# Attention scores and values on packed 32-wide TensorE tiles, in one burst per head, in place of whole-array matmuls spread among the projections

## The chip, the cores and the metric

The kernel runs on one core of one Trainium2 chip. The metric is device time in microseconds (us); lower is better. Executions of one kernel agree within about 0.2%. A profile is one execution taken by the hardware profiler. Its engines are PE (TensorE matmuls), PEld (TensorE weight loads, which overlap PE), DVE (VectorE), ACT (ScalarE), POOL (GpSimd) and SP (SyncE). `L630` is line 630 of that kernel's source, so the same statement has different line numbers in the two kernels. All runs told here were in the fast state, with the mean granted TensorE clock at 0.99 to 1.00. The 0.99 belongs to one experiment, in whose attention stage the clock halved for short stretches; this is told there.

## The reference, cut to what matters

```python
# S = 2048 tokens, 1024 wide; attention A: 32 heads of 128, segments of 32 tokens, 8 memory tokens; gated unit B: F = 3584
xn = layernorm(x)
s = A(xn, mem0, ...)     # per segment of 32: h = [mem (8), xs (32)]; q, k, v = h Wq, h Wk, h Wv
                         # p = softmax(mask(q k^T * scale)); o = p v; o Wo; its first 8 rows are the next memory
g = silu(B(xn, ...))     # (sigmoid(x w_gate) * (x w_up)) w_down
return x + s * g
```

The kernel does not run the 64 segments one after the other. It estimates the memories first, handles all segments at once, and checks at the end whether its estimate was good enough (a flag; if not, a sequential version follows). So a segment's attention is a causal 32x32 score block for its own keys, plus a memory term that is added to the values (`vm`) and to the denominator (a constant 8). The first segment keeps its own small 40x40 attention.

## The kernel before

For each head, TensorE computes q and k of all tokens: 2 x 5 blocks of about 411 columns, each with 8 matmuls, 80 in all ("projections", tile `pr`). The attention of the head before is spread among them. Four segments of 32 tokens share a 128x128 score matmul. Three quarters of its output lie outside the segments and are masked to zero.

```python
psb = es_p.enter_context(tc.tile_pool(name="psb", bufs=4, space=PSUM))     # shared matmul buffers, one bank each
...
        def s_steps(h, i):                                                  # scores: 16 matmuls a head, in batches of 4
            ...
            for j in range(n):
                o = M + (j0 + j) * P
                nc.tensor.matmul(s_ps[:, j * P:(j + 1) * P], lhsT=kt[:, o:o + P], rhs=qt[:, o:o + P], start=True, stop=True)
                if j < n - 1:
                    yield
            pv = pT[:, j0 * P:(j0 + n) * P]
            nc.scalar.activation(pv, s_ps[:, 0:n * P], ACTF.Exp, scale=scale)
            pv = pv.rearrange("p (a b) -> p a b", b=P)
            nc.vector.tensor_tensor(pv, pv, mask[:].unsqueeze(1).to_broadcast([P, n, P]), op=ALU.mult)
            yield

        def pv_steps(h, i):                                                 # values: 16 matmuls a head, 3 to a PSUM bank
            ...
            for j in range(n):
                o = (j0 + j) * P
                nc.tensor.matmul(o_ps[:, j, :], lhsT=pT[:, o:o + P], rhs=va[:, j0 + j, v0:v0 + OW],
                                 start=True, stop=True)                     # OW = 130: 128 values and ones for the denominator
            last = j0 + n == NT
            if last:                                                        # the first segment's own attention
                nc.tensor.matmul(o_ps[:, n, :], lhsT=pT[:, S:S + P], rhs=va[:, NT, v0:v0 + OW], start=True, stop=True)
            ...                                                             # VectorE: + vm, reciprocal, product, into osb

        for h in range(H + 1):                                              # cut
            for i in range(NSL):                                            # NSL = 80 projection matmuls
                ...
                if pj is not None:
                    next(pj, None)                                          # one projection matmul of head h
                if at is not None:
                    next(at, None)                                          # a step of the attention of head h - 1
```

After the last output tile, this kernel also runs 114 small matmuls on 32- and 64-wide tiles whose results nobody reads. They are a test of packed tiles that was left in:

```python
        X, Y, Z = wo_sb[:, 0, :], wo_sb[:, 1, :], wo_sb[:, 2, :]
        for _ in range(2):
            ...                                # 16 matmuls on 128x32 tiles (32 columns), 8 on 128x64 tiles (64 columns)
        ...
        for t in range(3):
            for c in range(4):
                for r in range(4):             # 48 matmuls on 32x32 tiles, 130 columns
                    q = slice(r * SEG, (r + 1) * SEG)
                    nc.tensor.matmul(pbs[r][c * SEG:(c + 1) * SEG, t * OW:(t + 1) * OW], lhsT=X[q, t * P + c * SEG:t * P + (c + 1) * SEG],
                                     rhs=Y[q, c * P:c * P + OW], start=True, stop=True)
```

## Time and profile before

| | before |
|---|---|
| median, us | 1582.82 (1582.62 to 1583.65, 4 runs) |
| span of the profile, us | 1581.1 |
| PE busy | 99% |
| distance of two heads in the attention stage, us | 15.79 |
| of this, 80 projections at 173.7 ns | 13.90 |
| attention matmuls of one head, us | 1.89 |
| last output matmul's start to the end, us | 8.40 |

The profile's page starts with the busy time and share of each engine.

```profile
PE 1567.0 (99%) x9353; PEld 808.9 (51%) x9456; DVE 708.5 (45%) x1252; ACT 539.7 (34%) x1087; POOL 162.4 (10%) x302
```

Its part on the chain that ended last gives shares of the span by engine, then by engine and line:

```profile
PE 99%; issue 0%; POOL 0%; ACT 0%; DVE 0%; POOLq 0%
PE pr L630 28%; PE a_ps L899 14%; PE v_ps L368 14%; PE y_ps L889 12%; PE u_ps L173 12%; PE g_ps L169 12%; PE o_ps L671 2%; PE s_ps L651 2%; PE acc L424 1%; PE vm_ps L533 1%; PE vm_ps L562 0%; PE pt L342 0%; PE o_ps L675 0%; POOL mx L434 0%; POOL mx L433 0%
```

The table by stretches of time shows that this holds inside the attention stage too: in 495 us PE is busy for all but 0.05 us, while VectorE and ScalarE have a quarter of their time or more to spare.

```profile
core 0: us, PE busy (x) PEld busy (x) DVE busy (x) ACT busy (x) POOL busy (x), PEclk, DMA share, GB/s
325.00:820.00 495.00, 494.95 (x3567) 302.95 (x3566) 361.39 (x688) 282.56 (x593) 57.22 (x107) 1.00 0.54 136
```

The timeline of PE in that stage (start in us, us, then the merged instructions) shows how attention is spread among projections. From one start to the next, two projections and one score take 0.40 us: 2 x 174 ns and 56 ns. Matmuls overlap, so durations (0.22 us for one score) must not be added. Starts are what counts.

```profile
612.82 0.22 PE L651 MATMUL s_ps<-qt,kt 128*128 128x128 bf16 x1
612.88 0.51 PE L630 MATMUL pr<-xnT,wqk 128*128 128x412 bf16 x2
613.23 0.22 PE L651 MATMUL s_ps<-qt,kt 128*128 128x128 bf16 x1
613.29 0.33 PE L671 MATMUL o_ps<-va,pT 128*128 128x130 bf16 x3
613.46 0.51 PE L630 MATMUL pr<-xnT,wqk 128*128 128x410 bf16 x2
```

At the end stands the left-over test. The timeline again; `128*32` and `32*32` are the tile shapes:

```profile
1572.84 0.28 PE L945 MATMUL pa<-wo_sb 128*32 128x32 bf16 x16
...
1573.05 0.32 PE L950 MATMUL pa<-wo_sb 128*64 128x64 bf16 x8
...
1574.69 0.60 PE L967 MATMUL pb<-wo_sb 32*32 32x130 bf16 x48
```

The starts of its single matmuls, read from the trace's records, price the packing:

```
128x32 tiles, 32 columns, ns from the first:  0 3 7 10 | 38 42 45 49 | 63 67 70 74 | 88 92 95 100
32x32 tiles, 130 columns, ns from the first:  0 3 6 10 ... 50 | 67 70 ... 117 | 252 261 269 277 ... 377
```

### The profile page before, as it was taken

Reading aid. Unit: us, or ns where it says so; the run is one execution under the profiler, and the core shown is the slowest. Engines: PE = TensorE matmul, PEld = TensorE weight load, DVE = VectorE, ACT = ScalarE, POOL = GpSimd, SP = SyncE. Lnnn points to the kernel's source line nnn. Section 1 sums busy time; section 2 is a strip of 40 time slices with the busy share of each in tenths; the row PEclk is TensorE's granted clock in tenths of the full one; section 3 lists DMA queues with packets and bytes.
Section 4 is the critical chain, followed back from the end, with each engine's and each line's share of the span. In section 5 each row is a group of like instructions: output and inputs, shape, how many; then the busy total and the mean of one; then the engine's idle time right before and its main releaser. Section 6 shows DMA issues by size and latency. Waiting matters only on the chain.

```text
span 1581.1 us, 22861 instructions
## 1 busy us (share of the span) xinstructions
PE 1567.0 (99%) x9353; PEld 808.9 (51%) x9456; DVE 708.5 (45%) x1252; ACT 539.7 (34%) x1087; POOL 162.4 (10%) x302
## 2 busy tenths in 40 slices
PE   9999999999999999999999999999999999999998
PEld 4444445566666666666654444444444444444444
DVE  6555534357777777777773112121223333311211
ACT  4555552155555555555541111111111122100000
POOL 2111110101101110111011101111100000000000
PEclk9999999999999999999999999999999999999999
DMA  7744654856564655455524353523253334343430
GB/s 228 206 140 140 207 187 141 247 129 156 157 166 124 157 158 139 108 142 148 112 61 147 129 184 127 201 79 98 62 136 104 93 117 107 103 122 88 109 102 29
DMA packets 257790, 212.99 MB, mean 135 GB/s; under 512 B 83528, under 2 KB 219848, under 8 KB 257680
## 3 DMA queue, kind: packets, MB, share of 16 engines
q1 hardware_dynamic: 229904, 140.40, 34.0%
q0 software_dynamic: 17200, 56.37, 10.0%
q10 hardware_dynamic: 10576, 14.70, 3.0%
q8 instruction: 76, 1.25, 0.3%
q14 instruction: 34, 0.28, 0.1%
HBM read 129.06 MB, written 63.50 MB: 122 GB/s over the span
## 4 chain that ended last, share of the span: by engine, by line
PE 99%; issue 0%; POOL 0%; ACT 0%; DVE 0%; POOLq 0%
PE pr L630 28%; PE a_ps L899 14%; PE v_ps L368 14%; PE y_ps L889 12%; PE u_ps L173 12%; PE g_ps L169 12%; PE o_ps L671 2%; PE s_ps L651 2%; PE acc L424 1%; PE vm_ps L533 1%; PE vm_ps L562 0%; PE pt L342 0%; PE o_ps L675 0%; POOL mx L434 0%; POOL mx L433 0%
## 5 line engine op out<-in xcount | busy, mean ns | idle before, releaser
L630 PE MATMUL pr<-xnT,wqk 128*128 128x412 bf16 (+1 forms) x2560 | 500.6, 337 | 0.0
L630 PEld LDWEIGHTS <-wqk 128*128 128x128 bf16 x2560 | 222.4, 97 | 134.3 <-issue 0.4
L899 PE MATMUL a_ps<-wo_sb,ot 128*128 128x512 bf16 (+2 forms) x1037 | 225.0, 372 | 1.0
L368 PE MATMUL v_ps<-wv_sb,xnT 128*128 128x512 bf16 x1002 | 222.2, 379 | 1.8 <-ACT xnT L344 0.7
L173 PE MATMUL u_ps<-xnT,wu 128*128 128x512 bf16 x879 | 210.3, 379 | 1.0
L169 PE MATMUL g_ps<-xnT,wg 128*128 128x512 bf16 x870 | 209.3, 379 | 1.3
L177 DVE SCALAR_TENSOR_TENSOR hst<-th,u_ps 128x512 bf16<-128x512 f32 x112 | 77.0, 687 | 286.5 <-PE u_ps L173 273.5
L889 PE MATMUL y_ps<-wd,ht 128*128 128x512 bf16 x877 | 197.2, 379 | 1.0
L176 ACT ACTIVATE th<-g_ps 128x512 f32<-128x512 f32 x112 | 67.0, 598 | 300.5 <-PE g_ps L169 287.0
L899 PEld LDWEIGHTS <-ot 128*128 128x128 bf16 x1056 | 102.1, 98 | 119.3
L368 PEld LDWEIGHTS <-xnT 128*128 128x128 bf16 x1024 | 99.4, 98 | 118.4 <-ACT xnT L344 1.2
L173 PEld LDWEIGHTS <-wu 128*128 128x128 bf16 x896 | 87.7, 98 | 105.7
L889 PEld LDWEIGHTS <-ht 128*128 128x128 bf16 x896 | 87.1, 98 | 105.3 <-issue 1.2
L169 PEld LDWEIGHTS <-wg 128*128 128x128 bf16 x896 | 86.7, 98 | 101.5
L680 DVE TENSOR_TENSOR of<-o_ps,vm 128x387 f32<-128x387 f32 x192 | 98.8, 515 | 42.5 <-PE o_ps L671 29.4
L633 ACT CAST kt<-pr 128x412 bf16<-128x412 f32 (+1 forms) x160 | 80.0, 500 | 92.9 <-PE pr L630 92.6
L655 ACT ACTIVATE pT<-s_ps 128x512 bf16<-128x512 f32 x128 | 76.4, 597 | 102.0 <-PE s_ps L651 101.1
L371 ACT CAST v_sb<-v_ps 128x512 bf16<-128x512 f32 x128 | 74.9, 585 | 104.9 <-PE v_ps L368 101.4
L651 PE MATMUL s_ps<-qt,kt 128*128 128x128 bf16 x512 | 110.4, 219 | 0.0
L892 ACT ACTIVATE th<-y_ps 128x512 f32<-128x512 f32 x32 | 19.1, 597 | 234.7 <-PE y_ps L889 234.7
L905 DVE SCALAR_TENSOR_TENSOR tmp<-a_ps,gq 128x512 f32<-128x512 f32 (+2 forms) x33 | 22.3, 675 | 166.7 <-PE a_ps L899 166.5
L633 ACT CAST qt<-pr 128x412 bf16<-128x412 f32 (+1 forms) x160 | 79.5, 497 | 27.5 <-PE pr L630 27.5
(165 smaller groups left out, 1155.6 us busy)
## 6 DMA issues: line engine op xcount, KB each, us to landing
vp_dram<-v_sb POOLq DMA_DIRECT2D x64, 256.0 KB, 3.3
va<-vp_dram SPq DMA_DIRECT2D x16, 1024.0 KB
o_dram<-osb POOLq DMA_DIRECT2D x16, 960.0 KB, 11.6
hT_dram<-hst POOLq DMA_DIRECT2D x56, 256.0 KB, 3.9
ht<-hT_dram SPq DMA_DIRECT2D x16, 896.0 KB, 5.1
vm<-vm_dram SPq DMA_DIRECT2D x48, 256.0 KB, 11.7
xt<-in_A_x_dram SPq DMA_DIRECT2D x32, 256.0 KB, 4.3
wo_t<-in_A_Wo_dram ACTq DMA_DIRECT2D x8, 1024.0 KB, 5.7
```

The costliest lines, as they stand in the source:

```text
L169: nc.tensor.matmul(g_ps[:], lhsT=wg[:, c, fc * P:(fc + 1) * P], rhs=xnT[:, c, tb * TB:(tb + 1) * TB], start=(c == 0), stop=(c == KC - 1))
L173: nc.tensor.matmul(u_ps[:], lhsT=wu[:, c, fc * P:(fc + 1) * P], rhs=xnT[:, c, tb * TB:(tb + 1) * TB], start=(c == 0), stop=(c == KC - 1))
L177: nc.vector.scalar_tensor_tensor(hst[:, :, fc, :], th[:].rearrange("p (a b) -> p a b", b=P), 1.0, u_ps[:].rearrange("p (a b) -> p a b", b= ...
L368: nc.tensor.matmul(v_ps[:], lhsT=xnT[:, c, t * P:(t + 1) * P], rhs=wv_sb[:, c, cg * 512:(cg + 1) * 512], start=(c == 0), stop=(c == KC - 1))
L371: nc.scalar.copy(v_sb[:, j * 512:(j + 1) * 512], v_ps[:])
L630: nc.tensor.matmul(pr[:, 0:b - a], lhsT=w_[:, c, hc], rhs=xmT[:, c, a:b], start=(c == 0), stop=(c == KC - 1))
L633: nc.scalar.copy(dst[:, a:b], pr[:, 0:b - a])
L651: nc.tensor.matmul(s_ps[:, j * P:(j + 1) * P], lhsT=kt[:, o:o + P], rhs=qt[:, o:o + P], start=True, stop=True)
L655: nc.scalar.activation(pv, s_ps[:, 0:n * P], ACTF.Exp, scale=scale)
L680: nc.vector.tensor_tensor(of[:, o:o + n, :], o_ps[:, 0:n, f:f + DH + 1], vm[:, j0:j0 + n, v0 + f:v0 + f + DH + 1], op=ALU.add)
L889: nc.tensor.matmul(y_ps[:], lhsT=hts[t][:, c, :], rhs=wd[:, c, hf * 512:(hf + 1) * 512], start=(c == 0), stop=(c == FC - 1))
L899: nc.tensor.matmul(a_ps[:], lhsT=ox[t][0][:, h, :], rhs=wo_sb[:, h, a:b], start=(h == 0), stop=(h == H - 1))
```

## The change

Its intent is to stop paying for the three quarters of each score matmul that are masked away. Segments are regrouped so that four of them (one from each quarter of the tokens) stand in the four 32-row groups of one 128x512 tile. Scores run on 128x32 column tiles, four at a time. Values run on 32x32 tiles, sixteen at a time. Exponentials and masks then touch 512 columns a head in place of 2048. All attention matmuls of a moment stand together in one burst: the scores of head h-1 and the values of head h-2, after the eighth projection of head h. Denominators get matmuls of their own (four of 4 columns). The value output takes four PSUM banks, so the shared buffers fall from four to three. The left-over test goes. Some loads move, and the memory term is loaded from a rearranged copy in larger packets.

```diff
-    psb = es_p.enter_context(tc.tile_pool(name="psb", bufs=4, space=PSUM))
+    psb = es_p.enter_context(tc.tile_pool(name="psb", bufs=3, space=PSUM))
...
+        def scores(h):
+            ...
+            xs = xss["s"] = psb.tile([P, 512], F32, name="xs", tag="big")
+            nc.tensor.matmul(xs[:, 0:L], lhsT=kt[:, 0:P], rhs=qt[:, 0:L], start=True, stop=True)
+            s_ps = ps.tile([P, PW], F32, name="s_ps", tag="s")
+            for t in range(NT):
+                for a in range(4):
+                    o = M + a * 4 * P + t * SEG
+                    nc.tensor.matmul(s_ps[a * SEG:(a + 1) * SEG, t * SEG:(t + 1) * SEG], lhsT=kt[:, o:o + SEG],
+                                     rhs=qt[:, o:o + SEG], start=True, stop=True)
...
+        def values(h):
+            ...
+            o_ps = ps.tile([P, 4, 4, DH], F32, name="o_ps", tag="o")
+            for q in range(4):
+                for c in range(4):
+                    t = 4 * q + c
+                    for a in range(4):
+                        r = slice(a * SEG, (a + 1) * SEG)
+                        nc.tensor.matmul(o_ps[c * SEG:(c + 1) * SEG, a, q, :], lhsT=pT[r, t * SEG:(t + 1) * SEG],
+                                         rhs=va[r, t, hc], start=True, stop=True)
+            xs = xss["v"] = psb.tile([P, 512], F32, name="xs", tag="big")
+            den = xs[:, 0:NT].rearrange("p (a q) -> p a q", q=4)
+            for q in range(4):
+                nc.tensor.matmul(den[:, :, q], lhsT=pT[:, q * P:(q + 1) * P], rhs=bones[:], start=True, stop=True)
+            nc.tensor.matmul(xs[:, P:P + OW], lhsT=pT[:, PW:PW + P], rhs=vx[:, v0:v0 + OW], start=True, stop=True)
...
-        for h in range(H + 1):
+        for h in range(H + 2):
...
+                if i == KC:
+                    if 0 < h <= H:
+                        scores(h - 1)
+                    if h > 1:
+                        values(h - 2)
+                    if 0 < h <= H:
+                        weights(h - 1)
+                    if h > 1:
+                        outputs(h - 2)
+                    if 0 < h <= H:
+                        causal(h - 1)
...
-            y_ps = psb.tile([P, 512], F32, name="y_ps", tag="big")
+            y_ps = ps.tile([P, 512], F32, name="y_ps", tag="y", bufs=2)
...
-        X, Y, Z = wo_sb[:, 0, :], wo_sb[:, 1, :], wo_sb[:, 2, :]
-        ...                                     (the whole left-over test)
```

## The prediction

> **What bounds the kernel.** TensorE. The page gives PE 99% of the 1581.1 us span, and the chain of waits is 99% PE. In the attention stage (table by stretches, 325 to 820 us) PE is busy 494.95 of 495.00 us at clock 1.00; DVE 361 and ACT 283 are not limits. So only PE time counts. Cheaper DVE masking, fewer exponentials and larger vm packets are off the critical path.
>
> **What attention costs PE now.** In the timeline one head takes 15.79 us start to start. Its 80 projection matmuls are 173.7 ns apart: 13.90 us. The other 1.89 us is attention: 16 score matmuls (56 ns apart), 17 value matmuls (57 ns), one 128x40 (26 ns).
>
> **What the change does.** Per head, one burst replaces these: a 128x40 matmul; 64 score matmuls on 128x32 column tiles, 32 columns each; 64 value matmuls on 32x32 tiles, 128 columns each; four 4-column denominator matmuls; one 130-column matmul. The kernel before ends with a probe of just such tiles, and its timeline prices them:
> - 128x32 tiles, 32 columns: four start within 10 ns, the next four 25 ns later. 64 cost about 0.41 us.
> - 32x32 tiles, 130 columns: 32 start within 117 ns, then 135 ns of nothing, then one each 8.3 ns. I read this as a full queue of 64 instructions that empties, then a dispatch limit near 4.15 ns per instruction.
> - Changing tile shape costs about 100 ns each time (106 to 149 ns between starts, against 25 to 55 within a shape). The Trainium skill ("TensorEngine Tiling (Array Packing)", Tiling Modes) says a change of mode drains the engine; this trace agrees. A burst has three changes.
>
> Estimate of a burst: 0.03 + 0.12 + scores 0.41 + 0.06 (queue empty) + 0.05 (dispatch) + 0.11 + values 0.43 + 0.14 + denominators 0.11 + 0.06 = 1.52 us. So 1.52 us replaces 1.89 us: 0.37 us a head, 12 us over 32 heads. The small pairs are bound by dispatch and three drains.
>
> **Tail.** The probe goes. Its PE work runs from 1572.84 to 1575.3 us. PE alone then reads the flag and branches (4.27 us), and the last barrier waits for that, so the probe is on the critical path: 2.3 us saved. The output DMA lands by 1574.7 us, early enough.
>
> **Other.** Three projection buffers instead of four: matmul groups take 1.4 to 1.7 us, copies 0.5 to 0.7 us, so no waits. Each head's chain now stretches over three heads, leaving slack. I allow 1 us for a stall at the stage's start, where the memory layout moves.
>
> **Prediction: 1569 us, 80% range 1561 to 1577.** Chances: faster by over 2% 0.03, within 2% 0.94, slower by over 2% 0.03.
>
> **What would show it.** Heads 15.4 us apart; PE still 99%; projections still 174 ns apart; bursts near 1.5 us with three gaps near 0.1 us; score tiles 6 to 8 ns apart on average, value tiles about 8 ns once the queue is empty; DVE and ACT busy less without effect; last PE matmul followed directly by the branch.
>
> **What would make it wrong.** Instruction fetch: a burst has about 270 instructions and the program is fetched in 16 KB pieces taking 1 to 2 us; starving would push bursts over 2 us and eat the gain. Faster dispatch than 8.3 ns a pair would bring bursts to 1.2 us (1559 us). Waits on the single score and output buffers, or a projection buffer held by VectorE, would appear as gaps after the burst.

## The result, and the profile after

| | before | after |
|---|---|---|
| median, us | 1582.82 (1582.49 to 1584.96, 12 runs) | 1569.42 (1568.86 to 1570.14, 8 runs) |
| span of the profile, us | 1581.1 | 1568.4 |
| distance of two heads, us | 15.79 | 15.45 |
| attention matmuls of one head, us | 1.89 | 1.54 |
| last output matmul's start to the end, us | 8.40 | 5.86 |

The ratio is 0.9914 (95% interval 0.9904 to 0.9924). Ratios here are the mean time of one kernel's fast runs over that of the other's of the same rounds, so they are not quite the ratio of the medians quoted. The change is 0.9% faster, which is clear of noise.

PE is still the only limit. The page's engine line, and the chain:

```profile
PE 1553.2 (99%) x12438; PEld 789.2 (50%) x12542; DVE 641.5 (41%) x964; ACT 492.4 (31%) x991; POOL 152.9 (10%) x299
```

```profile
PE 98%; DVE 1%; DMA 1%; issue 0%; ACT 0%; SPq 0%
```

The table by stretches: the same full PE, with nearly twice the matmuls, and 60 us less VectorE and 44 us less ScalarE.

```profile
325.00:820.00 495.00, 494.89 (x6772) 290.99 (x6773) 301.46 (x416) 239.06 (x504) 49.21 (x110) 1.00 0.57 138
```

The timeline of PE over one burst, with the projections left out, and the start of the next head's burst:

```profile
512.29 0.18 PE L652 MATMUL xs<-qt,kt 128*128 128x40 bf16 x1
512.40 0.66 PE L657 MATMUL s_ps<-qt,kt 128*32 128x32 bf16 x64
513.00 0.73 PE L685 MATMUL o_ps<-va,pT 32*32 32x128 bf16 x64
513.66 0.26 PE L690 MATMUL xs<-bones,pT 128*128 128x4 bf16 x4
513.78 0.22 PE L691 MATMUL xs<-vx,pT 128*128 128x130 bf16 x1
...
527.74 0.18 PE L652 MATMUL xs<-qt,kt 128*128 128x40 bf16 x1
```

The starts of the single matmuls of one such burst, from the trace's records:

```
ns from the burst's start
small whole-array matmul   0
scores, 64                 112 ... 590     first four within 10 ns, then four each 25 ns; from the 33rd on one each 8.4 ns
values, 64                 705 ... 1215    first 31 within 141 ns; the 33rd 251 ns after the first; then one each 8.3 ns
denominators, 4            1370 ... 1460
first segment              1485
next projection            1541
```

Where the 12.7 us of the two profiles went, by starts on PE:

| stretch | before, us | after, us | difference |
|---|---|---|---|
| start to last value projection | 238.28 | 238.53 | +0.25 |
| from there to the first q/k projection | 73.34 | 73.91 | +0.57 |
| first to last q/k projection | 503.34 | 491.76 | -11.58 |
| from there to the first output matmul (last heads, gated unit) | 340.49 | 341.06 | +0.57 |
| first to last output matmul | 417.24 | 417.24 | 0.00 |
| last output matmul to the end | 8.40 | 5.86 | -2.54 |

The fourth line belongs to attention as well: the values of the last head now follow the projections. So attention gave 11.0 us, which is 0.344 us a head. The tail gave 2.5 us, and 0.8 us came on before the stage. The first line varies from run to run: in the changed kernel run again it was 239.17 us, because that run's first loads came later (the view of waits has 1.8 us for a load of `wv_sb`, against 0.3 us).

The second line has a new wait. The view of waits (engine and line, what it waited for, us in total, times, longest) lists it for the kernel after. The kernel before has no such line.

```profile
PE g_ps L169 <- DVE hst L177: 0.4, 1, 0.4
```

### The profile page after: what moved, and what is told of

Read it like the earlier page. It is cut to its first block, busy times and chain, and to the rows that moved or that the text cites. A ratio compares the mean times of both kernels' runs of the same rounds, so it can differ in the third digit from the quotient of the medians.

```text
span 1568.4 us, 28695 instructions
## 1 busy us (share of the span) xinstructions
PE 1553.2 (99%) x12438; PEld 789.2 (50%) x12542; DVE 641.5 (41%) x964; ACT 492.4 (31%) x991; POOL 152.9 (10%) x299
## 4 chain that ended last, share of the span: by engine, by line
PE 98%; DVE 1%; DMA 1%; issue 0%; ACT 0%; SPq 0%
PE pr L641 28%; PE a_ps L916 14%; PE v_ps L372 14%; PE y_ps L906 12%; PE u_ps L173 12%; PE g_ps L169 12%; PE o_ps L685 1%; PE s_ps L657 1%; PE acc L433 1%; PE vm_ps L542 0%; DMA wv_sb<-in_A_Wv_dram 0%; PE vm_ps L571 0%; PE xs L690 0%; DVE svT L391 0%; DMA xt<-in_A_x_dram 0%
## 5 line engine op out<-in xcount | busy, mean ns | idle before, releaser
L641 PE MATMUL pr<-xnT,wqk 128*128 128x412 bf16 (+1 forms) x2560 | 450.2, 337 | 0.0
L641 PEld LDWEIGHTS <-wqk 128*128 128x128 bf16 x2560 | 248.2, 97 | 191.0 <-issue 0.4
L710 DVE TENSOR_TENSOR osb<-of,rden 128x1024 bf16<-128x1024 f32 x64 | 78.4, 1225 | 2.1
L624 DVE TENSOR_TENSOR mx<-mx,ab 128x2048 bf16<-128x2048 bf16 x64 | 78.2, 1222 | 1.2
L709 DVE TENSOR_TENSOR of<-o_ps,vm 128x1024 f32<-128x1024 f32 x64 | 77.5, 1211 | 0.0
```

The source lines that it names most:

```text
L624: nc.vector.tensor_tensor(mx[:, x, :], mx[:, x, :], abs_.pop((h, x))[:], op=ALU.max)
L641: nc.tensor.matmul(pr[:, 0:b - a], lhsT=w_[:, c, hc], rhs=xmT[:, c, a:b], start=(c == 0), stop=(c == KC - 1))
L709: nc.vector.tensor_tensor(of[:], o_ps[:, 2 * i:2 * i + 2].rearrange("p a q d -> p (a q) d"), vm[:, x, hc], op=ALU.add)
L710: nc.vector.tensor_tensor(osb[:, x, hc], of[:], rd[:, x].unsqueeze(2).to_broadcast([P, 8, DH]), op=ALU.mult)
```

## The experiments

All ten kernels gave results within tolerance, even the one ("only the scores packed") whose denominators belong to other segments on purpose. Three (the tail alone, the work given back, values ahead of scores) were timed together with the changed kernel run again, on the same chip, so it and the kernel before of that group (1582.94 us) are their yardsticks. The others ran in two more groups on two other chips, where the kernel before took 1583.18 and 1582.82 us; they are held against the changed kernel's 1569.42 us.

### The changed kernel again

> The changed kernel again, unedited, as the yardstick of this group of runs. Expected 1569.4 us within 1 us. It also tells whether the start of the program, where its profile was 0.25 us behind the kernel before by the end of the value projections, varies from run to run.

Measured: 1569.53 us (1568.78 to 1571.28, 5 runs), ratio to before 0.9917 (0.9904 to 0.9931). The last value projection started at 239.17 us, against 238.53 in the first profile. Over the twelve profiles told here it lies between 238.13 and 240.42 us, so the start alone can move one profile by up to 2 us. Heads were 15.45 us apart and bursts 1.540 us, as in the first profile.

### The tail alone

```diff
 # the kernel before
-        X, Y, Z = wo_sb[:, 0, :], wo_sb[:, 1, :], wo_sb[:, 2, :]
-        ...                                     (the whole left-over test)
```

> The kernel before, without the packed test matmuls at its end. Theory (TensorE alone reads the flag, branches and releases the last barrier, so the test is on the critical path): the time falls by 2.3 to 2.6 us, to about 1580.4 us. Rival (the last output transfer would end as late anyway): it falls by under 0.5 us. The two profiles put the step from the last output matmul to the end at 8.40 us before and 5.86 us after, 2.54 us less; if this kernel shows about 5.9 us, the tail is explained by the test alone.

Measured: 1580.03 us (1579.58 to 1580.48, 5 runs) against 1582.94 us, 2.9 us less; ratio 0.9982 (0.9968 to 0.9995). From the last output matmul to the end its profile has 5.42 us. The test was on the critical path, and the rival falls. The trace's records of the kernel before show why: TensorE reads the flag at 1575.05 us, when its last test matmul starts, and its branch then takes 4.27 us. SyncE has finished its waits for transfers by 1575.2 us and then stands in the last barrier (4.26 us in one wait) until TensorE arrives.

### VectorE and ScalarE given their work back

```diff
 # the changed kernel; scr and scd are scratch tiles of 128x512
+                if i in (26, 38, 48, 56, 68) and 0 < h < H:
+                    if i < 50:
+                        nc.scalar.activation(scr[:], scr[:], ACTF.Exp, scale=scale)
+                    nc.vector.tensor_tensor(scd[:], scd[:], scd[:], op=ALU.mult)
```

> The changed kernel with useless work given back to VectorE (five 128x512 multiplies a head, about 2 us) and ScalarE (three 128x512 exponentials a head, about 1.8 us), as much as the change took from them. Theory (they are off the critical path): the time stays at 1569.4 us within 1 us, heads stay 15.45 us apart, and the busy times of VectorE and ScalarE in the attention stage return to about 360 and 290 us. Rival (part of the gain came from relieving them): at least 3 us slower.

Measured: 1569.62 us (1568.84 to 1569.65, 5 runs), ratio to before 0.9915. Heads are 15.44 us apart. Its table by stretches shows the work back at 357 and 288 us, with PE unmoved:

```profile
325.00:820.00 495.00, 494.89 (x6771) 290.86 (x6772) 356.81 (x572) 288.26 (x597) 49.41 (x110) 1.00 0.57 138
```

So none of the gain came from the fewer exponentials and masks.

### Only the scores packed

```diff
 # the changed kernel
-                    o = M + a * 4 * P + t * SEG
+                    o = M + t * P + a * SEG
...
+            for a in range(4):                      # spread the masked weights block-diagonally (VectorE)
+                r = slice(a * SEG, (a + 1) * SEG)
+                nc.vector.tensor_copy(bds[h % 2][r, :, r], pv[r])
...
-            for q in range(4):                      # 64 value matmuls on 32x32 tiles
-                ...
+            for t in range(NT):                     # 16 value matmuls on the whole array
+                nc.tensor.matmul(o_ps[:, t // 4, t % 4, :], lhsT=bds[h % 2][:, t, :], rhs=va[:, t, hc], start=True, stop=True)
```

(The values are also loaded in natural order, in one transfer.)

> The changed kernel with the value half of the packing undone: weights spread into block-diagonal 128x128 tiles by four VectorE copies a head, then 16 whole-array value matmuls of 128 columns as before; one change of tile shape less. Its denominators belong to other segments on purpose, so the result may be wrong. Theory (sum of the parts measured so far): 0.11 + scores 0.48 + change 0.14 + 16 x 0.056 + denominators and first segment 0.19 = 1.81 us a burst against 1.54, so 0.27 us more a head, about 1578 us: the value packing is worth three quarters of the gain and the score packing alone little, since each pays for its own drains. Rival (packing the values gains nothing, as its 64 pairs at 8.3 ns and its drain cost as much as 16 whole matmuls): 1569.4 us within 2 us.

Measured: 1576.61 us (1576.29 to 1576.83, 4 runs) against 1583.18 us for the kernel before, ratio 0.9958 (0.9941 to 0.9975). A burst is 1.770 us, 0.23 us more than with both packed. With the tail's 2.9 us taken off, packing the scores alone is worth about 3.7 us, net of the denominators' own matmuls, and packing the values as well about 7.2 us more (1576.61 to 1569.42 us). Gathering the matmuls in one burst is no gain of its own here: the 16 whole-array value matmuls of this burst start 56 ns apart, against 57 ns in the kernel before. Packing the values alone was not run. The rival (the values gain nothing) falls. The two are not independent: the whole-array value matmuls need the way back from the score tiles too (117 ns from the last score to the first of them).

### One more change of tile shape

```diff
 # the changed kernel, in scores(h)
-            nc.tensor.matmul(xs[:, 0:L], ...)       # before the score tiles
             ...                                     # 64 score tiles
+            nc.tensor.matmul(xs[:, 0:L], ...)       # after them, before the value tiles
```

> The changed kernel with the one small whole-array matmul of a burst moved from before the score tiles to between score and value tiles: the same matmuls, one more change of tile shape. Theory (each change drains the engine): whole array after the column tiles costs about 0.15 us, the small matmul 0.03 us, the change to 32x32 tiles 0.11 us as now: about 0.15 us more a head, 5 us in all, about 1574 us. Rival (changes are hidden by the pipeline): 1569.4 us.

Measured: 1572.46 us (1572.38 to 1572.82, 4 runs), ratio to before 0.9933 (0.9916 to 0.9950). That is 3.0 us more than the changed kernel (1569.42 us), where 5 were expected. Bursts rose from 1.540 to 1.644 us, 0.104 us each. The trace has the pieces: column tiles to the small matmul 116 ns, that to the value tiles 122 ns, in place of 115 ns directly; and the first change, now straight from a projection, 19 ns cheaper. So a change of shape does cost about 0.1 us and is not hidden. The expectation had 0.15 us for the way back to the whole array, which was too much.

### Values ahead of scores

```diff
 # the changed kernel: order on TensorE
-scores(h - 1): small matmul, 64 score tiles;  values(h - 2): 64 value tiles, denominators, first segment
+values(h - 2): 64 value tiles;  scores(h - 1): 64 score tiles;  denominators, first segment (h - 2); small matmul (h - 1)
```

> The changed kernel with the value tiles ahead of the score tiles in each burst, and the whole-array matmuls together at the end. Theory (a window of 64 instructions runs at once, then dispatch gives one pair each 8.3 ns, and dispatch goes on while a change of tile shape drains): values then take 112 + 251 + 31 x 8.3 ns, the drain before the scores hides behind dispatch, and the last score starts about 60 ns earlier than the last value does now; with a shorter last drain the burst falls from 1.54 to about 1.45 us, 0.09 us a head, 2.9 us in all: about 1566.5 us. Rival (the cost of a burst is a sum of parts that does not depend on their order): 1569.4 us, unchanged.

Measured: 1570.04 us (1569.23 to 1571.01, 5 runs) beside 1569.53 us for the changed kernel of the same group: no gain, where the theory promised 2.9 us. The starts, by record:

```
                      values: first ... 33rd ... last     scores: first ... 33rd ... last
as changed                    0 ... 252  ... 510                  0 ... 216  ... 477
values first                  0 ... 252  ... 510                  0 ... 217  ... 477
```

Each section costs the same wherever it stands. So the step "dispatch goes on while the shape changes, and shortens what follows" is wrong. The row order below shows what sets the 33rd pair.

### Another order of the value tiles

```diff
 # the changed kernel, in values(h)
-            for q in range(4):
-                for c in range(4):
-                    t = 4 * q + c
-                    for a in range(4):
-                        r = slice(a * SEG, (a + 1) * SEG)
+            for a in range(4):
+                r = slice(a * SEG, (a + 1) * SEG)
+                for q in range(4):
+                    for c in range(4):
+                        t = 4 * q + c
```

> The changed kernel with the 64 value tiles of a head in another order: all of one row group before the next, so that only 4 of the 16 tiles are in use at a time. Theory (64 instructions in flight, then one pair each 8.3 ns, and within one row group the four tiles stream 128 columns together in about 55 ns): 16 groups of 55 ns, 0.88 us in place of 0.51 us, so 0.37 us more a head, about 1581 us. Rival (the gap of 251 ns between the first and the third use of a tile is a limit of the tile's weights): two groups each 251 ns, 2.0 us, so 1.5 us more a head, about 1616 us. Second rival (only the number of instructions counts): 1569.4 us.

Measured: 1574.06 us (1573.48 to 1575.01, 4 runs), ratio to before 0.9944 (0.9927 to 0.9960): 4.6 us more than the changed kernel, 0.133 us a burst. All three expectations missed the time. The trace still separates two of them:

- A tile's third use starts 66 ns after its first (its fourth 120 ns), not 251 ns. So 251 ns is no limit of a tile's weights, and that rival falls.
- The 33rd pair again starts 251 ns after the first, though the tiles come in another order. The first value matmul of these bursts lasts 225 ns in the records.

In three kinds of section the 33rd pair starts 26 to 28 ns after the end of the section's first matmul: 225 + 26 = 251 ns here and in the changed kernel, 190 + 26 = 216 ns for the scores, 198 + 26 = 224 ns for the 64-column values of the next experiment. (The profiler models the ends of matmuls, so this rests on modelled ends; the starts are recorded.) Thirty-two pairs are 64 instructions. This is what one sees if 64 instructions may be in flight, and each finished one lets the next in. The Trainium skill gives TensorE an engine queue depth of 64 ("TensorE: Matmul & The Clock Gate", the table at its top); these numbers agree. What makes one row group's tiles slower than 8.3 ns a pair (groups about 56 ns apart, but eight starts in one, where I had expected four) was not settled.

### Twice the pairs for the same columns

```diff
 # the changed kernel, in values(h)
             for q in range(4):
+                for b in range(2):
+                    e = slice(hh * DH + b * 64, hh * DH + (b + 1) * 64)
                 ...
-                        nc.tensor.matmul(o_ps[c * SEG:(c + 1) * SEG, a, q, :], lhsT=..., rhs=va[r, t, hc], ...)
+                            nc.tensor.matmul(o_ps[c * SEG:(c + 1) * SEG, a, q, b * 64:(b + 1) * 64], lhsT=..., rhs=va[r, t, e], ...)
```

> The changed kernel with each value matmul of 128 columns split into two of 64 columns, on the same weights loaded twice: the same columns, 64 more pairs of weight load and matmul a head. Theory (dispatch of about 4.15 ns an instruction bounds a burst): 64 x 8.3 ns = 0.53 us more a head, 17 us in all, about 1586 us, and the steady distance of value matmuls stays 8.3 ns. Rival (streaming of columns bounds it): 1569.4 us, with the distance falling to about 4 ns.

Measured: 1626.56 us (1624.26 to 1629.78, 4 runs), ratio to before 1.0274 (1.0257 to 1.0292). This is 57 us over the changed kernel, where dispatch alone should give 17. Half of the bursts do what dispatch predicts: 17 of 31 last between 2.017 and 2.23 us (one of 0.71 us has no values yet), and pairs stay 8.3 ns apart though they carry half the columns. Streaming as the bound is ruled out. The rest last up to 4.53 us. Their timeline has a hole whose cause the profile calls "issue", which means no wait that it can see:

```profile
390.08 0.18 PE L652 MATMUL xs<-qt,kt 128*128 128x40 bf16 x1
390.19 0.66 PE L657 MATMUL s_ps<-qt,kt 128*32 128x32 bf16 x64
390.78 1.17 PE L687 MATMUL o_ps<-va,pT 32*32 32x64 bf16 x123
393.89 0.21 PE L687 MATMUL o_ps<-va,pT 32*32 32x64 bf16 x5 [1.93 <-issue]
394.03 0.26 PE L692 MATMUL xs<-bones,pT 128*128 128x4 bf16 x4
```

The view of waits sums the larger ones:

```profile
PE o_ps L687 <- issue: 21.5, 12, 2.3
PE pr L641 <- issue: 2.8, 3, 1.8
PE xs L692 <- issue: 2.2, 1, 2.2
```

In the trace's DMA records TensorE's program comes in packets of 16384 bytes. In the attention stages of four of these kernels there is one for each 254 to 261 of TensorE's instruction records, so I take a packet as 256 instructions. In the attention stage there were 16 distances of over 0.45 us between starts. Each ended 1.2 to 1.6 us after such a packet had landed. A burst here has 396 instructions, against 268 in the changed kernel. The count of instructions bears this out. Take the instructions that TensorE has started, less 256 for each packet that has landed. Just before the landing that ended the distance, this difference was the same, to the instruction, in 12 of the 16 (in the other four it was smaller). So TensorE had then run through all that it had been given. In the changed kernel the difference stays at least 27 instructions below that.

So the 57 us are 14.3 us of dispatch (30 bursts of 0.476 us), 25.7 us of holes in bursts and 16.7 us of longer distances among the projections. Of these 16.7 us, 3.2 us are three more holes, and 13.2 us are the clock. The trace's clock records show eight stretches of 3.41 us at half clock (0.50), each beginning 0.3 to 1.6 us after the end of a distance of 2.1 to 2.5 us, and there projections start about 342 ns apart. Four more distances of over 2 us are not followed by one, and neither the changed kernel nor the next one has any in this stage. The table by stretches shows it, after the hole that ended at 411.89 us (10 and 19 matmuls in 3 us; PEclk, third from the end, is 0.50 and then 1.00):

```profile
413.00:416.00 3.00, 3.00 (x10) 1.35 (x9) 2.97 (x4) 0.50 (x1) 0.81 (x2) 0.50 0.86 243
417.00:420.00 3.00, 3.00 (x19) 1.68 (x18) 2.59 (x3) 1.22 (x3) 0.00 (x0) 1.00 0.61 181
```

### Twice the pairs, but in two places

```diff
 # the kernel with twice the pairs: 64 value pairs with the scores, the other 64 with the denominators 28 projections later
+                if i == (36 if h < H else 24) and h > 1:
+                    values(h - 2, 1)
+                    outputs(h - 2)
```

> The kernel with twice the value pairs again, but its second 64 value pairs of a head moved 28 projection matmuls later, so that a burst has at most about 260 instructions and the sequencer can fetch in between. It does more work in changes of shape than e4 (two more a head). Theory (the 1 to 2.5 us gaps of e4 are instruction fetches of 16 KB that a burst of about 400 instructions outruns): no gaps over 0.3 us in a burst, heads about 0.75 us further apart than in the changed kernel (0.51 us for 64 pairs, 0.25 us for the two changes), about 1594 us, some 30 us faster than e4 in spite of more changes. Rival (more pairs or more changes cost by themselves): slower than e4, over 1626 us.

Measured: 1591.05 us (1590.84 to 1591.75, 4 runs), ratio to before 1.0051 (1.0036 to 1.0066): 35.5 us faster than with all pairs in one place, in spite of two more changes of shape a head. Heads are 16.11 us apart, 0.66 us more than in the changed kernel (0.75 expected). In the whole stage one hole was left, of 0.7 us. More pairs do not by themselves cost what the experiment above showed. The holes are the program's instructions not being there in time, and with the long holes the stretches at half clock are gone too.

### Three shared buffers alone

```diff
 # the kernel before
-    psb = es_p.enter_context(tc.tile_pool(name="psb", bufs=4, space=PSUM))
+    psb = es_p.enter_context(tc.tile_pool(name="psb", bufs=3, space=PSUM))
...                                             (and the gated unit's and the down projection's buffers as in the change;
                                                 12 of the left-over test's 48 last matmuls are dropped for want of a buffer)
```

> The kernel before with the change's PSUM split alone: three shared matmul buffers in place of four, and two of its own for the down projection (one group of the closing test is left out for want of buffers). Both profiles of the changed kernel show a wait of 0.4 us of a gate matmul on VectorE near 246 us, which the kernel before has not. Theory (the third buffer short causes it): the same wait shows here, the projections of the attention stage start about 0.6 us later, and the time rises by 0.3 to 0.7 us, within noise. Rival (it comes from elsewhere in the change): no such wait.

Measured: 1584.70 us (1584.48 to 1586.48, 5 runs) against 1582.82 us, ratio 1.0010 (0.9997 to 1.0024). The interval spans 1, though each of the five runs is longer than each of the nine of the kernel before. The profile is clearer. Its view of waits has the line sought, and the stretch from the last value projection to the first q/k projection is 73.90 us, as in the changed kernel (73.91) and not as before (73.34). It has a second wait, of 1.0 us at the start of the attention stage, which the changed kernel does not show; why only this one has it was not tested.

```profile
PE pr L630 <- DVE vm_sb L569: 1.0, 1, 1.0
...
PE g_ps L169 <- DVE hst L177: 0.4, 1, 0.4
```

All ten profiles with three buffers have 73.88 to 73.91 us there, and both with four have 73.34 us. So the fourth buffer was worth about 0.6 us before the stage. This profile's first stretch was also 2.1 us longer than that of the kernel before (240.42 us), the longest of the twelve; it has a wait of 1.8 us for a load there and 3.41 us at half clock near its start.

## Why the prediction was right

The predicted 1569 us met 1569.42 us. The mechanism was right, but so close a hit was partly luck: the gain of attention was put 1 us too high, that of the tail 0.2 to 0.6 us too low, and 1 us was allowed for a stall that did not come where it was expected. Point by point:

- **"TensorE ... So only PE time counts": right.** PE stays at 99%. Giving VectorE and ScalarE their work back changed nothing (1569.62 us).
- **"1.52 us replaces 1.89 us: 0.37 us a head, 12 us over 32 heads": right, a little high.** A burst is 1.541 us, and attention gave 0.344 us a head, 11.0 us. Term by term, in us:

| term | predicted | measured |
|---|---|---|
| small matmul and change to column tiles | 0.03 + 0.12 | 0.112 |
| 64 scores, with the queue running empty | 0.41 + 0.06 | 0.478 |
| change to 32x32 tiles, with some dispatch | 0.05 + 0.11 | 0.115 |
| 64 values | 0.43 | 0.510 |
| change to the whole array | 0.14 | 0.155 |
| denominators | 0.11 | 0.115 |
| first segment | 0.06 | 0.056 |
| sum | 1.52 | 1.541 |

- **The mis-sized term is the values.** I let the instructions that dispatch supplies during the change shorten the section. The reordered kernels show that they do not: the 33rd pair waits until the section's first matmul is through, 251 ns after its start, whatever stood in the queue, and 31 x 8.33 ns follow. The left-over test had already shown this: 252 ns and 31 x 8.3 ns make 509 ns for 64 pairs. Two smaller errors the other way, in the first two changes of shape, made up for it by luck (0.038 and 0.045 us against 0.080 us).
- **"A full queue of 64 instructions that empties, then a dispatch limit near 4.15 ns per instruction": it fits.** The 33rd pair is late in every section and in every order tried. With half the columns the pairs stay 8.3 ns apart. That these are 4.15 ns for each of a pair's two instructions was not tested. What empties and refills was pictured too simply, as just said.
- **"Changing tile shape costs about 100 ns each time": right.** It was 112, 115 and 155 ns between starts in the changed kernel, and a fourth change cost 0.104 us. (The first 112 ns include the small matmul. In the left-over test the changes took 106 to 171 ns; the prediction's "106 to 149" leaves out its last two.) The Trainium skill's statement that a change of mode drains the engine ("TensorEngine Tiling (Array Packing)", Tiling Modes) agrees with these.
- **"2.3 us saved" in the tail: right, a little low.** The two profiles give 2.54 us, and the kernel before without its test was 2.9 us faster. With the test gone, TensorE is no longer alone at the end: in the changed kernel it leaves its branch at 1566.35 us, and SyncE starts its own last waits at 1566.01 us. What SyncE waits for first are the last two output transfers, whose last updates came at 1565.99 and 1566.21 us. So little more is to be gained at the end by TensorE alone.
- **"Three projection buffers ... so no waits": wrong by 0.6 us.** For the projections it holds. But the same buffers serve the gated unit's matmuls among the memory work ahead of the stage, and there one gate matmul waits 0.4 us for VectorE. The kernel before with three buffers has the same wait. The 1 us allowed for "a stall at the stage's start, where the memory layout moves" covered this by luck, for another reason.
- **Instruction fetch, named as the main risk: real, but not reached.** Bursts of 268 instructions showed no hole, with 27 instructions to spare by the count above. Bursts of 396 lost about 42 us over the stage: 29 us of holes and 13 us of half clock after them.

## What to carry to other kernels

Packing small matmuls trades array time for instructions. Here a run of 64 tile pairs started 32 of them within its first matmul's latency and then one each 8.3 to 8.4 ns, whether they carried 32, 64 or 128 columns, plus about 0.1 us for each change of tile shape (and an order that kept to one row group at a time cost 0.13 us a burst more); price these first, because here they left 0.35 us of gain a head where the masked-away three quarters of the score arithmetic suggest far more. Count the instructions of a burst as well: 268 at one place ran clean but close to the edge, 396 stalled for up to 2.5 us at a time and then partly ran on at half clock, and splitting them over two places cured nearly all of it. With TensorE 99% busy, work taken off VectorE and ScalarE bought nothing here; and left-over work at the very end (2.5 us of it here) cost its full length, because its engine still had to take part in the last barrier.

## What the Trainium skill lacked or had wrong

- "TensorE: Matmul & The Clock Gate", Part 3, gives starts of about 4 ns for packed tiles (3.4 ns here agrees), but not that this holds for 32 pairs only: the 33rd started 26 to 28 ns after the first's modelled end (251, 224 and 216 ns after its start in three kinds of section), and from there on pairs came 8.3 ns apart.
- The same page, Part 1, says that start-to-start never drops below about 25 ns. That fits whole-array matmuls of 4 columns (25 ns here), not matmuls on different tiles (3.4 to 8.3 ns), for which the page's Part 3 has its own figure.
- "TensorEngine Tiling (Array Packing)" says that a change of mode drains the engine, without a price: 112 to 155 ns between starts here.
- "Runtime: NRT & Kernel Launch", Instruction fetch mechanics, calls the cost of crossing a 16 KiB boundary mostly hidden. The packets of 16384 bytes agree. But bursts of 396 small TensorE instructions had holes of up to 2.5 us, 29 us in the attention stage; at 268 instructions there were none. The section's 128 KiB of instruction memory for TensorE (2048 instructions) does not look compatible with holes after 396: by the count of packets against instructions told above, TensorE never had more than about 540 instructions ahead of it (an estimate: the difference told above runs over about 540 instructions from just after a landing to the count at which TensorE ran dry).
- The latter section warns of taken branches, without a price: TensorE's branch past the unused fallback took 3.6 to 4.3 us at the end of the twelve profiles. A packet of 16384 bytes landed 1.4 us before it ended, both before and after the change, which agrees.
